# Chunk 0's statistics by quarters, two of its tiles staged by ScalarE, and transposes inside dense groups that read half of the chunk

## Chip, cores, metric

One core of one Trainium2 chip. The metric is the device time of one execution in microseconds; lower is better. Every timed comparison is of runs of two kernels on the same chip in the same rounds, with a 95% interval. Below, a "ratio" is the mean time of one kernel's runs over the mean of the other's runs of the same rounds; it is not quite the ratio of the medians that are quoted beside it. The record calls two kernels the same where they differ by less than 2%.

## The reference

Four residual layers over a sequence of 2048 tokens of width 1024, in bf16: a spectral layer (A) and a dense layer (B), twice.

```python
x = x + A(layernorm(x))      # rfft2 over (2048, 1024), times a complex filter, irfft2
x = x + B(layernorm(x))      # mish(x @ w1 + b1) @ w2, hidden width 3584
x = x + A(layernorm(x))
x = x + B(layernorm(x))
```

## The kernel before

Layer B works on four chunks of 512 tokens, each of four tiles of 128 tokens. What matters here is the passage from A to B, which occurs twice in an execution. In it, TensorE does the last stage of the inverse transform (`i4`, 128 small matmuls for tiles 0 to 3 and 128 for tiles 4 to 15), the results are added to the residual stream `XS` or staged in `YS`, VectorE takes the layer-norm statistics, scales a tile (`apply`), TensorE transposes it (`transposed`) and VectorE copies the transposed tile out of PSUM (the memory, in banks, into which TensorE writes) into `XT`, which the first product (`mm1`) then reads.

In these traces each engine keeps its program order: in the changed kernel below, the square root is ready to run at 620.08 us and starts at 620.51, behind ScalarE's own copies. The helper `op` makes an instruction wait for whatever wrote what it reads; `writes` also waits for earlier readers.

```python
def i4(self, lo, nb, u0, n, bank):          # n lanes of the inverse transform for nb tiles
    ...
    self.group(fns, reads=[... self.r_mt], writes=self.r_bank[bank:bank - (-n // k)])

def i4_out(self, lo, nb, u0, n, bank, staged=None):
    ...
    if staged is None:                      # VectorE adds PSUM to XS
        self.op(self.dve, ... tensor_tensor(xs, src, xs, ALU.add), reads=rb, parts=...)
    else:                                   # ScalarE copies PSUM to YS
        self.op(self.act, ... activation(dst, src, ACT.Copy), reads=rb, parts=[staged.res])

def transposed(c, t, xn, eng=None):
    bank = 6 + nt[0] % 2                    # banks 6 and 7 in turn
    ...                                     # 8 transposes of 128x128 into the bank
    self.op(eng or dve, fn, reads=[self.r_bank[bank]], parts=[XT[c % 2].res])

def mm1(c, fg, half=None):                  # 256 hidden columns; half: 256 of 512 tokens
    ...
    for fl in range(2):                     # banks 0 to 2 in turn
        ...
        self.group(fns, reads=[wb.res, x.res], writes=[self.r_bank[bank]])
        self.op(act, ... ACT.Mish ..., reads=[self.r_bank[bank], self.r_b1], writes=[ra])

# ---- the passage
for u in range(4):
    self.i4(0, 4, 32 * u, 32, 2 * u)
    self.i4_out(0, 4, 32 * u, 32, 2 * u)    # VectorE, four tiles at a time
rest(0)                                     # 15 lanes of tiles 4-15, banks 0-2, ScalarE stages
rest(3)                                     # the same in banks 3-5
self.stats_dve(0)
self.stats_dve(1)
for j in range(2):
    self.root(j, 1)                         # square root on ScalarE, reciprocal on VectorE
    xn[j] = self.apply(j)
rest(0)
late = rest(3, evac=False)
self.warm(ACT.Mish)                         # ScalarE's table load
for j in range(2):
    transposed(0, j, xn[j])
late()
...
for fg in range(4):
    mm1(0, fg, 0)
    rest(3)
for j in (2, 3):
    transposed(0, j, xn[j])
mm1(0, 0, 1)
rest(3)
...
mm1(0, 4)
for j in (4, 5):
    transposed(1, j - 4, xn[j])
...
for fg in range(2):
    mm1(1, fg, 0)
for j in (6, 7):
    transposed(1, j - 4, xn[j])
for fg in range(2):
    mm1(1, fg, 1)
# from here on full groups of mm1, then mm2; gapless
```

## Time and profile before

| | before |
|---|---|
| median of 3 runs, later of 4 | 1028.27 us, 1028.76 us |
| span of the profiled run | 1031.2 us |
| TensorE busy | 92% of the span |
| first passage: first `i4` matmul to first `mm2` matmul | 117.6 us |
| second passage | 120.3 us |

The passage is the measure I use throughout: the start of the first `mm2` matmul (L1024 before, L1046 in the changed kernel) less the start of the first `i4` matmul (L926 before, L939 after), read from TensorE's timeline. Before: 237.75 - 120.11 and 737.71 - 617.46. In a line of a timeline the first number is the start in us, the second the duration, then engine, line and operation, and in brackets the engine's idle time just before it and what ended it. The second passage's first group of `mm1`, 16 matmuls, in TensorE's timeline of the kernel before:

```profile
629.22 3.60 PE L1007 MATMUL PS<-ARENA 128*128 128x256 bf16 x16 [0.79 <-DVE ARENA L982]
```

The same group in the first passage (131.46 us) took 1.92 us: in the second the clock was at half. Where a text below says that the clock fell, the granted clock of short windows went from 1.00 to 0.50, for about 3.4 us ("one window") or about 6.8 us ("two windows", 627.3 to 634.1 us here). A waits line reads: who waited, for whom, us in total, times, longest.

### The profile page before, as it was taken

How to read it: one execution, taken by the hardware profiler on the slowest of the kernel's cores; microseconds unless marked ns; L12 is line 12 of the kernel's file. 1: busy time of each engine (PE TensorE's matmuls, PEld its weight loads, DVE VectorE, ACT ScalarE, POOL GpSimd, SP SyncE). 2: the span in 40 equal slices, each digit the busy share in tenths (PEclk: the TensorE clock that was granted, in tenths of full speed). 3: DMA queues.
4: the chain of work that ended last, by engine and by line, in shares of the span. 5: the costliest groups of instructions: out<-in, count | busy, mean ns of one | idle time of the engine just before them, and what ended most of it. 6: DMA issues, size and time to landing. Idle time of an engine off the chain costs nothing.

```text
span 1031.2 us, 13517 instructions
## 1 busy us (share of the span) xinstructions
PE 947.1 (92%) x5695; PEld 505.6 (49%) x5777; DVE 332.6 (32%) x682; ACT 348.5 (34%) x487; POOL 73.3 (7%) x114
## 2 busy tenths in 40 slices
PE   0799599999999999999979958999999999999998
PEld 0567475444444444444446747644444444444443
DVE  6897469002333100033346836840011100000111
ACT  6989384441000333300019846544200023330000
POOL 3342000000000000002511100000000000000000
PEclk9999799999999999999989988999999999999999
DMA  9879713653111220002932874155611122200000
GB/s 285 206 245 303 195 50 93 204 191 113 46 46 35 72 82 21 1 21 75 195 67 77 231 187 123 42 173 185 181 25 45 45 74 71 62 1 10 21 21 31
DMA packets 153052, 106.98 MB, mean 104 GB/s; under 512 B 74384, under 2 KB 132064, under 8 KB 152992
## 3 DMA queue, kind: packets, MB, share of 16 engines
q1 hardware_dynamic: 141472, 77.04, 26.4%
q0 software_dynamic: 9488, 27.68, 9.3%
q10 hardware_dynamic: 2032, 1.39, 0.5%
q8 instruction: 46, 0.75, 0.3%
q14 instruction: 14, 0.11, 0.0%
HBM read 80.85 MB, written 20.71 MB: 98 GB/s over the span
## 4 chain that ended last, share of the span: by engine, by line
PE 85%; DVE 7%; ACT 5%; DMA 2%; issue 1%; ACTq 0%; DVEq 0%
PE PS L1007 38%; PE PS L1024 37%; PE PS L676 2%; PE PS L750 2%; DVE BN L460 2%; PE PS L771 2%; ACT ARENA L601 2%; ACT ARENA L757 1%; ACT ARENA L728 1%; DVE XS L946 1%; PE PS L926 1%; DMA ARENA<-u_scratch 1%; DVE ARENA L982 1%; ACT ARENA L711 1%; PE PS L789 1%
## 5 line engine op out<-in xcount | busy, mean ns | idle before, releaser
L1007 PE MATMUL PS<-ARENA 128*128 128x512 bf16 (+1 forms) x1950 | 390.3, 359 | 9.0 <-DVE ARENA L982 7.2
L1024 PE MATMUL PS<-ARENA 128*128 128x512 bf16 x1756 | 385.5, 379 | 1.9
L1011 ACT ACTIVATE ARENA<-PS,B 128x512 bf16<-128x512 f32 (+1 forms) x248 | 159.3, 645 | 417.9 <-PE PS L1007 417.8
L1007 PEld LDWEIGHTS PS<-ARENA 128*128 128x128 bf16 x1984 | 193.9, 98 | 201.4 <-DVE ARENA L982 8.6
L1024 PEld LDWEIGHTS PS<-ARENA 128*128 128x128 bf16 x1792 | 175.4, 98 | 211.4
L1029 DVE TENSOR_TENSOR XS<-PS,XS 128x512 bf16<-128x512 f32 x64 | 44.3, 692 | 593.9 <-PE PS L1024 593.9
L460 DVE BATCH_NORM_STATS2 BN<-XS 128x6 f32<-128x512 bf16 x108 | 69.6, 674 | 7.5 <-DMA XS<-in_A_x_dram 6.4
L926 PE MATMUL PS<-MT,ARENA 128*128 128x32 bf16 (+1 forms) x512 | 22.2, 202 | 17.9 <-DMA ARENA<-u_scratch 15.6
L750 PE MATMUL PS<-ARENA 128*128 128x256 bf16 x256 | 32.3, 273 | 4.7 <-DVE ARENA L739 3.2
L676 PE MATMUL PS<-FD,ARENA 128*128 128x256 bf16 (+1 forms) x256 | 33.1, 278 | 3.8 <-DVE ARENA L603 1.5
L757 ACT ACTIVATE ARENA<-PS 128x1024 bf16<-128x1024 f32 x32 | 33.4, 1071 | 7.5 <-PE PS L750 7.5
L432 ACT ACTIVATE RS<-MV,EPS 128x1 f32<-128x1 f32 (+1 forms) x7 | 2.1, 295 | 100.0 <-DVE MV L463 96.4
L949 ACT ACTIVATE ARENA<-PS 128x1440 bf16<-128x1440 f32 (+2 forms) x20 | 25.0, 1274 | 28.1 <-PE PS L926 28.1
L728 ACT ACTIVATE ARENA<-PS 128x1024 bf16<-128x1024 f32 x32 | 33.0, 1061 | 4.0 <-PE PS L724 4.0
L249 POOL DMA_DIRECT2D xn_scratch<-ARENA x12 | 6.5, 541 | 378.5 <-DVE ARENA L499 378.5
L750 PEld LDWEIGHTS PS<-ARENA 128*128 128x128 bf16 x256 | 24.2, 98 | 12.6 <-DVE ARENA L739 4.6
L926 PEld LDWEIGHTS PS<-MT,ARENA 128*128 128x128 bf16 x512 | 20.3, 104 | 20.0 <-issue 15.9
L676 PEld LDWEIGHTS PS<-FD,ARENA 128*128 128x128 bf16 x256 | 25.1, 101 | 8.8 <-DVE ARENA L603 3.1
L771 PE MATMUL PS<-ARENA,BD 128*128 128x256 bf16 x192 | 27.1, 288 | 2.3 <-ACT ARENA L757 2.3
L732 DVE TENSOR_TENSOR ARENA<-ARENA 128x1024 bf16<-128x1024 bf16 x32 | 22.1, 689 | 20.8 <-ACT ARENA L728 20.8
L799 ACT ACTIVATE ARENA<-PS 128x1024 bf16<-128x1024 f32 x24 | 24.8, 1073 | 3.7 <-PE PS L771 3.7
L711 ACT ACTIVATE ARENA<-PS 128x1024 bf16<-128x1024 f32 x22 | 23.0, 1055 | 7.3 <-PE PS L676 7.3
(70 smaller groups left out, 499.2 us busy)
## 6 DMA issues: line engine op xcount, KB each, us to landing
ARENA<-in_B_w_dram SPq DMA_DIRECT2D x56, 512.0 KB, 4.0
ARENA<-in_B_w_dram SPq DMA_DIRECT2D x56, 256.0 KB, 4.4
u_scratch<-ARENA SPq DMA_DIRECT2D x14, 512.0 KB, 3.6
ARENA<-u_scratch SPq DMA_DIRECT2D x14, 512.0 KB, 5.7
XS<-in_A_x_dram SPq DMA_DIRECT2D x4, 1024.0 KB, 8.7
w_scratch<-ARENA POOLq DMA_DIRECT2D x8, 512.0 KB, 5.6
ARENA<-w_scratch POOLq DMA_DIRECT2D x8, 512.0 KB, 4.6
out_dram<-XS SPq DMA_DIRECT2D x16, 256.0 KB, 2.0
```

Source lines behind the costliest of these rows:

```text
L460: self.op(self.dve, lambda e: e.bn_stats(self.BN[:, j, 6 * h:6 * h + 6], self.XS[:, j, 512 * h:512 * h + 512]), reads=[self.r_xs[j]], part ...
L676: fns.append(lambda e: e.matmul(dst, at(r), FD[:, t:t + n], start=start, stop=stop))
L711: self.op(act, lambda e: e.activation(dst, src, ACT.Copy), reads=banks, parts=[za.res, zb.res])
L728: self.op(act, lambda e: e.activation(x.ap.rearrange("p a b -> p (a b)"), ps, ACT.Copy, scale=SIG), reads=banks, writes=[x.res])
L750: fns.append(lambda e, c=c, part=part: e.matmul(ps[:, c * 256:(c + 1) * 256], yk.ap[:, part, c * P:(c + 1) * P], t[:, (128, 0)[part]:(384, ...
L757: self.op(act, lambda e: e.activation(v.ap[:, :, i, :], src, ACT.Copy), reads=banks, parts=[v.res])
L771: fns.append(lambda e, dst=dst, part=part, c=c: e.matmul(dst, BD[:, c:c + P], mov(kd, part), start=(part == 0), stop=(part == 1)))
L926: fns.append(lambda e, l=l: e.matmul(self.PS[:, bank + l // k, l % k * w:(l % k + 1) * w], self.UT.ap[:, u0 + l, :], self.MT[:, 8 * lo:8 * ...
L1007: fns.append(lambda e, db=db, bank=bank, fl=fl: e.matmul(PS[:, bank, 0:w], wb.ap[:, db, fl * P:(fl + 1) * P], x.ap[:, db, tok], start=(db ...
L1011: self.op(act, lambda e, bank=bank, ft=ft: e.activation(at.ap[:, ft, tok], PS[:, bank, 0:w], ACT.Mish, bias=self.B1[:, ft:ft + 1]), reads= ...
L1024: fns.append(lambda e, i=i, ft=ft: e.matmul(PS[:, bank, :], at.ap[:, ft, t * P:(t + 1) * P], W2[ft].ap[:, h * 512:(h + 1) * 512], start=(i ...
L1029: self.op(dve, lambda e: e.tensor_tensor(xs, PS[:, bank, :], xs, ALU.add), reads=[self.r_bank[bank]], writes=[self.r_xs[j]])
```

## The change

The intent: have chunk 0's statistics ready sooner, by halving VectorE's adds (ScalarE stages tiles 2 and 3 in a new buffer `YC`) and taking statistics a quarter of the tile at a time between the adds; and let no copy of transposed tiles keep TensorE waiting, by putting the transposes into the middle of a group of matmuls that reads only the half of the chunk that is ready.

```diff
+    def stats_quarter(self, j, u):
+        ...
+        x = self.XS[:, j, :].rearrange("p (h l) -> p h l", l=P)[:, :, 32 * u:32 * u + 32]
+        self.op(self.dve, lambda e: e.bn_stats(bn[:, 6 * u:6 * u + 6], x), reads=[self.r_xs[j]], parts=[r])
+        if u == 3:
+            t = self.op(self.dve, lambda e: e.bn_aggr(self.MV[:, j, :], bn), reads=[r], writes=[r])
 ... (i4_out: tiles=, prog=; a staged copy now writes its banks' record)
-                self.op(self.act, lambda e, ...: e.activation(dst, src, ACT.Copy), reads=rb, parts=[staged.res])
+                self.copy(prog or self.act, at(staged.ap), src, [], rb, parts=[staged.res])
 ... (XT: one record for each half of the chunk)
-            self.op(eng or dve, fn, reads=[self.r_bank[bank]], parts=[XT[c % 2].res])
+            self.op(eng or dve, fn, reads=[self.r_bank[bank]], parts=[r_xt[c % 2][t // 2]])
-        def mm1(c, fg, half=None):
+        def mm1(c, fg, half=None, mid=()):
             for fl in range(2):
+                if fl:
+                    for f in mid:
+                        f()
-                self.group(fns, reads=[wb.res, x.res], ...)
+                self.group(fns, reads=[wb.res] + (r_xt[c % 2] if half is None else [r_xt[c % 2][half]]), ...)
 ... (the passage)
         for u in range(4):
             self.i4(0, 4, 32 * u, 32, 2 * u)
-            self.i4_out(0, 4, 32 * u, 32, 2 * u)
+            self.i4_out(0, 4, 32 * u, 32, 2 * u, tiles=(0, 2))
+            self.i4_out(0, 4, 32 * u, 32, 2 * u, staged=YC, tiles=(2, 2))
+            for j in range(2):
+                self.stats_quarter(j, u)
         rest(0)
+        self.root(0, 2)
         rest(3)
-        self.stats_dve(0)
-        self.stats_dve(1)
         for j in range(2):
-            self.root(j, 1)
             xn[j] = self.apply(j)
-        rest(0)
-        late = rest(3, evac=False)
-        self.warm(ACT.Mish)
         for j in range(2):
             transposed(0, j, xn[j])
-        late()
+        rest(3)
+        self.warm(ACT.Mish)
 ...
         for fg in range(4):
-            mm1(0, fg, 0)
+            mm1(0, fg, 0, mid=turns(0, 2, 3) if fg == 3 else ())
             rest(3)
-        for j in (2, 3):
-            transposed(0, j, xn[j])
+            if fg == 2:
+                rest(6, 10, dve)
         mm1(0, 0, 1)
-        rest(3)
+        rest(3, 13)
 ...
         mm1(0, 4)
         at_tiles(1)
-        for j in (4, 5):
-            transposed(1, j - 4, xn[j])
+        mm1(0, 5, mid=turns(1, 0, 1))
+        for ft in range(4):
+            load_w2(ft)
 ...
         for fg in range(2):
-            mm1(1, fg, 0)
-        for j in (6, 7):
-            transposed(1, j - 4, xn[j])
+            mm1(1, fg, 0, mid=turns(1, 2, 3) if fg else ())
         for fg in range(2):
             mm1(1, fg, 1)
 ... (mm1(1, 2) alone; loads of W2 and residual adds moved accordingly)
```

More of the change, by code (lines that the diff above doesn't have):

```diff
@@ L463, in stats_half @@
             self.op(self.dve, lambda e: e.bn_aggr(self.MV[:, j, :], self.BN[:, j, :]), reads=[r], writes=[r])
+    def stats_quarter(self, j, u):
+        r = self.r_mv[j]
+        if u == 0:
+            r.begin()
+        bn = self.BN[:, 2 * j:2 * j + 2, :].rearrange("p a b -> p (a b)")
+        x = self.XS[:, j, :].rearrange("p (h l) -> p h l", l=P)[:, :, 32 * u:32 * u + 32]
+        self.op(self.dve, lambda e: e.bn_stats(bn[:, 6 * u:6 * u + 6], x), reads=[self.r_xs[j]], parts=[r])
+        if u == 3:
+            t = self.op(self.dve, lambda e: e.bn_aggr(self.MV[:, j, :], bn), reads=[r], writes=[r])
+            for i in range(4):
+                self.r_mv[i].r(self.dve, t)
     def stats_dve(self, j):
@@ L533, in pair, with copy @@
         return self.PS[:, 2 * i:2 * i + 2, :].rearrange("p a b -> p (a b)"), [self.r_bank[2 * i], self.r_bank[2 * i + 1]], 2 * i
-    def copy(self, prog, dst, src, reads, writes, scale=None):
+    def copy(self, prog, dst, src, reads, writes, scale=None, parts=()):
         if prog is self.act:
@@ L541, in copy @@
             fn = lambda e: e.tensor_copy(dst, src)
-        return self.op(prog, fn, reads=reads, writes=writes)
+        return self.op(prog, fn, reads=reads, writes=writes, parts=parts)
     def first_scales(self):
@@ L928, in i4, with i4_out @@
         self.group(fns, reads=self.r_ut[u0 // 32:(u0 + n - 1) // 32 + 1] + [self.r_mt], writes=self.r_bank[bank:bank - (-n // k)])
-    def i4_out(self, lo, nb, u0, n, bank, staged=None):
+    def i4_out(self, lo, nb, u0, n, bank, staged=None, prog=None, tiles=None):
         w = 8 * nb
         k = 512 // w
+        t0, tn = tiles or (0, nb)
         for b0, m, i in ((0, n // k, k), (n // k, 1, n % k)):
@@ L937, in i4_out @@
                 continue
-            src = self.PS[:, bank + b0:bank + b0 + m, 0:i * w].rearrange("p b (i c) -> p c b i", c=w)
+            src = self.PS[:, bank + b0:bank + b0 + m, 0:i * w].rearrange("p b (i c) -> p c b i", c=w)[:, 8 * t0:8 * (t0 + tn)]
             l = slice(u0 + b0 * k, u0 + b0 * k + m * i)
@@ L944, in i4_out @@
             if staged is None:
-                xs = at(self.XS[:, lo:lo + nb, :])
-                self.op(self.dve, lambda e, src=src, xs=xs: e.tensor_tensor(xs, src, xs, ALU.add), reads=rb, parts=self.r_xs[lo:lo + nb])
-            else:
-                dst = at(staged.ap)
-                self.op(self.act, lambda e, src=src, dst=dst: e.activation(dst, src, ACT.Copy), reads=rb, parts=[staged.res])
+                j = slice(lo + t0, lo + t0 + tn)
+                xs = at(self.XS[:, j, :])
+                self.op(self.dve, lambda e, src=src, xs=xs: e.tensor_tensor(xs, src, xs, ALU.add), reads=rb, parts=self.r_xs[j])
+            else:
+                self.copy(prog or self.act, at(staged.ap), src, [], rb, parts=[staged.res])
     def load_w1(self, after=()):
@@ L963, in layer_B @@
         base = 28 * li
-        XT, AT, r_at = [None, None], [None, None], [None, None]
+        XT, AT, r_xt, r_at = [None, None], [None, None], [None, None], [None, None]
         nt, nh, no = [0], [0], [0]
@@ L972, in transposed @@
                 if XT[c % 2] is None:
-                    XT[c % 2] = self.alloc(f"XT{c % 2}", self.ob[f"XT{c % 2}"], [8, 512])
-                XT[c % 2].res.begin()
+                    off = self.ob[f"XT{c % 2}"]
+                    XT[c % 2] = self.alloc(f"XT{c % 2}", off, [8, 512])
+                    r_xt[c % 2] = self.sub_res(XT[c % 2], f"xt{c % 2}h", 2, off, 8192)
+                for r in r_xt[c % 2]:
+                    r.begin()
             fns = []
@@ L989, in turned @@
             if t == 0:
-                x.res.begin()
+                for r in r_xt[c % 2]:
+                    r.begin()
             for db in range(8):
                 self.dma(sp, x.ap[:, db, t * P:(t + 1) * P], xn.ap[:, db * P:(db + 1) * P], f"xt{c % 2}_{t}", reads=[xn.res],
-                         parts=[x.res], transpose=True)
-        def mm1(c, fg, half=None):
+                         parts=[r_xt[c % 2][t // 2]], transpose=True)
+        def mm1(c, fg, half=None, mid=()):
             n = base + 14 * (c // 2) + fg
@@ L1008, in mm1 @@
                         PS[:, bank, 0:w], wb.ap[:, db, fl * P:(fl + 1) * P], x.ap[:, db, tok], start=(db == 0), stop=(db == 7)))
-                self.group(fns, reads=[wb.res, x.res], writes=[self.r_bank[bank]])
+                self.group(fns, reads=[wb.res] + (r_xt[c % 2] if half is None else [r_xt[c % 2][half]]), writes=[self.r_bank[bank]])
                 at, ra = AT[c % 2], r_at[c % 2][ft]
@@ L1059, in layer_B @@
         YS.res.begin()
+        YC = self.alloc("YC", self.ob["XT1"], [2, self.D])
+        YC.res.begin()
         xn = {}
-        for j in range(4):
+        for j in range(2):
             self.r_xs[j].begin()
@@ L1070, in at_tiles, with rest, turns @@
                 self.live.append((off + ft * 1024, off + ft * 1024 + 1024, r))
-        def rest(bank, evac=True):
-            u0, n = self.u0, min(15, P - self.u0)
+        def rest(bank, n=15, prog=act):
+            u0 = self.u0
             self.u0 += n
             self.i4(4, 12, u0, n, bank)
-            out = lambda: self.i4_out(4, 12, u0, n, bank, staged=YS)
-            if not evac:
-                return out
-            out()
+            self.i4_out(4, 12, u0, n, bank, staged=YS, prog=prog)
         def residual(j):
-            self.op(dve, lambda e: e.tensor_tensor(self.XS[:, j, :], self.XS[:, j, :], YS.ap[:, j - 4, :], ALU.add),
-                    reads=[YS.res], writes=[self.r_xs[j]])
+            y, i = (YS, j - 4) if j > 3 else (YC, j - 2)
+            self.op(dve, lambda e: e.tensor_tensor(self.XS[:, j, :], self.XS[:, j, :], y.ap[:, i, :], ALU.add),
+                    reads=[y.res], writes=[self.r_xs[j]])
+        def turns(c, *ts):
+            return [lambda t=t: transposed(c, t, xn[4 * c + t]) for t in ts]
         self.u0 = 0
@@ L1090, in layer_B @@
             self.i4(0, 4, 32 * u, 32, 2 * u)
-            self.i4_out(0, 4, 32 * u, 32, 2 * u)
+            self.i4_out(0, 4, 32 * u, 32, 2 * u, tiles=(0, 2))
+            self.i4_out(0, 4, 32 * u, 32, 2 * u, staged=YC, tiles=(2, 2))
+            for j in range(2):
+                self.stats_quarter(j, u)
         rest(0)
+        self.root(0, 2)
         rest(3)
-        self.stats_dve(0)
-        self.stats_dve(1)
         for j in range(2):
-            self.root(j, 1)
             xn[j] = self.apply(j)
-        rest(0)
-        late = rest(3, evac=False)
-        self.warm(ACT.Mish)
         for j in range(2):
             transposed(0, j, xn[j])
-        late()
+        rest(3)
+        self.warm(ACT.Mish)
         at_tiles(0)
-        self.stats_dve(2)
-        self.stats_dve(3)
+        for j in (2, 3):
+            residual(j)
+            self.stats_dve(j)
         self.scales(2, 2)
@@ L1138, in layer_B @@
         for fg in range(2):
-            mm1(1, fg, 0)
-        for j in (6, 7):
-            transposed(1, j - 4, xn[j])
+            mm1(1, fg, 0, mid=turns(1, 2, 3) if fg else ())
         for fg in range(2):
             mm1(1, fg, 1)
-        w2_order = list(range(16)) + list(range(16, 28))
-        for fg in range(5, 14 + 3):
+        mm1(1, 2)
+        w2_order = list(range(4, 28))
+        for fg in range(6, 14 + 3):
             if fg < 14:
@@ L1149, in layer_B @@
             mm1(1, fg - 3)
-            if fg < 9:
-                for j in (2 * fg - 2, 2 * fg - 1):
+            if fg < 10:
+                for j in (2 * fg - 4, 2 * fg - 3):
                     residual(j)
```

## The prediction

> **What bounds the kernel now.** I read the page first (shares of busy time, then the chain), then the chain in order of time to find the stretches in which TensorE does not set the end, then the timelines of TensorE, VectorE and ScalarE there, then the granted clock in short windows.
>
> The page: TensorE (PE) is busy for most of the span, and the two lines of the dense layer hold three quarters of the chain.
>
> ```profile
> PE 947.1 (92%) x5695; PEld 505.6 (49%) x5777; DVE 332.6 (32%) x682; ACT 348.5 (34%) x487; POOL 73.3 (7%) x114
> PE PS L1007 38%; PE PS L1024 37%; PE PS L676 2%; PE PS L750 2%; DVE BN L460 2%; PE PS L771 2%; ACT ARENA L601 2%; ACT ARENA L757 1%; ACT ARENA L728 1%; DVE XS L946 1%; PE PS L926 1%; DMA ARENA<-u_scratch 1%; DVE ARENA L982 1%; ACT ARENA L711 1%; PE PS L789 1%
> ```
>
> The change touches only the passage from the spectral layer to the dense layer, twice per execution (from 120 us and from 617 us). The chain through the first passage (start, length, what):
>
> ```profile
> 120.11 1.03 PE PS L926 x32
> 121.16 4.63 DVE XS L946 x4
> 125.82 1.30 DVE BN L460 x2
> 127.35 1.16 DVE BN L460 x2
> 128.97 1.64 ACT ARENA L949
> 130.63 1.28 ACT L425
> 132.13 1.27 ACT ARENA L949
> ...
> 141.90 1.30 DVE ARENA L982 x2
> ...
> 154.88 1.30 DVE ARENA L982 x2
> 156.23 3.67 PE PS L1007 x32
> 160.38 1.30 DVE ARENA L982 x2
> ```
>
> The reader sees four adds (L946), the statistics of tiles 0 and 1 (L460), ScalarE's evacuations and its table load, and then three times 1.30 us in which VectorE copies two transposed tiles (L982) while TensorE has nothing to do. TensorE's waits from 113 to 240 us confirm the last point:
>
> ```profile
> PE PS L1007 <- DVE ARENA L982: 3.6, 4, 0.9
> ```
>
> TensorE's own timeline gives the durations I use below:
>
> ```profile
> 133.45 0.81 PE L926 MATMUL PS<-MT,ARENA 128*128 128x96 bf16 x15
> 134.09 1.91 PE L1007 MATMUL PS<-ARENA 128*128 128x256 bf16 x16
> 154.22 1.08 PE L977 MATMUL PS<-IDENT,ARENA 128*128 128x128 bf16 x16
> ```
>
> Start to start, 15 lanes of the remaining inverse transform ("a rest", L926) take 0.64 us (43 ns a lane), a half group of 16 matmuls of 256 columns takes 1.75 us, a full one 3.46 us (16 of 216 ns: 49 take 10.74 us less the drain), and two tiles of transposes 0.92 us. From about 165 us on TensorE is gapless (72.6 of 73 us), so only these passages can give. All useful TensorE work between 120.1 and 165.2 us is about 38 us, so even a perfect passage would save some 7 us, 14 us in both: under 1.5%.
>
> The second passage repeats the first but is 2.6 us longer by the time chunk 0's second half starts (643.22 - 617.46 against 143.24 - 120.11). The reason is the clock:
>
> ```profile
> 625.00:627.00 2.00, 0.67 (x15) 0.53 (x13) 1.89 (x7) 0.90 (x3) 0.00 (x0) 1.00 1.16 311
> 627.00:629.00 2.00, 1.41 (x15) 0.96 (x12) 1.56 (x3) 1.98 (x2) 0.00 (x0) 0.58 1.18 299
> 629.00:631.00 2.00, 1.78 (x9) 1.28 (x10) 1.97 (x5) 1.73 (x3) 0.00 (x0) 0.50 0.93 236
> 631.00:633.00 2.00, 2.00 (x14) 1.50 (x13) 1.78 (x8) 0.62 (x2) 0.00 (x0) 0.50 0.06 17
> ```
>
> After a thin stretch (0.67 us of TensorE in two) the clock (column before the DMA share) falls to 0.50 and the first matmul groups run at half speed.
>
> **What the Trainium skill says.** (1) "TensorE: Matmul & The Clock Gate", Part 1: full clock after a busy window of about 3.4 us, half clock after an idle one, in windows that run freely. The trace agrees on both passages (0.50 at the first matmuls, the fall at 627.3, the rise near 634.1, two windows apart), except that here a window need not be idle to cost the clock: I count about 1.3 us of work in the one before 627.3. (2) "VectorE: DVE Perf Modes", section on the errata: an fp32 tensor_tensor takes (N+151)/0.96 ns. The trace: 1216 ns for N = 1024, 692 for 512, so halving the add halves little less than its time. (3) "ScalarE: Activation LUTs", What ACT_TABLE_LOAD costs: 186 + 0.833 N ns with overlap of about 93; the trace has 1408 ns for 1440 elements and 592 for 480, so about 0.62 us for 512. (4) "PSUM — Partial Sum Buffer", Terms: two engines on one bank at once collide. No run here shows it, but the diff obeys it: an evacuation now writes its bank's record, so ScalarE's copy of tiles 2 and 3 waits until VectorE's add of tiles 0 and 1 has left the same banks.
>
> **Part 1: statistics by quarters.** Removed from VectorE: two of the four tiles in each of four adds (1.16 us each start to start), and the statistics after them (4 of 0.65 us and two aggregations). Added: four adds of 512 elements, 0.69 us + 0.03 to the dependent instruction; eight statistics of 256 elements, about 0.41 us each by itself (674 ns less 256/0.96) and 0.35 start to start. A quarter cycles in 0.72 + 2 x 0.35 = 1.42 us. Add number 3 starts at 121.16 + 3 x 1.42 = 125.44 and ends at 126.13; the last aggregation ends near 127.4, against 128.74: 1.35 us earlier. But ScalarE is a strict queue: its fourth staged copy can start only at 126.17, then comes the rest's evacuation (about 1.25 start to start) and only then the square root: 126.17 + 0.54 + 1.25 = 127.96, not 127.4. Reciprocal, scaling: first transpose at 129.05 against 129.40, second tile's copy ends at about 131.05, first matmul group at 131.10 against 131.46. Of 1.35 us some 0.36 remain.
>
> **Part 2: one rest goes behind the transposes and before the table load.** Its evacuation can start at 130.75 and ends at 132.2; table load and warm-up end at 133.65; Mish 0 ends at 134.1, Mish 1 at 134.5, and the next evacuation at 135.9. TensorE, through with groups 0 and 1 at 135.25, waits for that bank set until 135.95 (0.7 us lost). The kernel before is at the same place at 135.84, with one rest more behind it in fact, though the new one gives ten lanes to VectorE later. The 0.36 us are gone.
>
> **Part 3: chunk 0's tiles 2 and 3 inside group 3.** The wait of 0.94 us at 143.24 goes: the last rest (0.64) and half a group lie over the copies. But the ten lanes for VectorE use banks 6 and 7, which the transposes need next. From 139.43: copy of 960 elements about 1.16 us, from 139.6 to 140.77, while TensorE has only 0.87 us of work to 140.3: it waits 0.5. Then 0.92 + 0.87 + 0.64 us: chunk 0's second half starts at 143.24, as before. The last rest has 13 lanes instead of 8: +0.21, so 145.55 against 145.34.
>
> **Part 4: chunk 1's transposes inside groups.** Before: the two waits for VectorE's copy after 154.22 and 159.73 cost 1.09 and 1.11 us, and the transposes themselves wait 0.16 us. After: from 145.55, three half groups 5.24, full groups 4 and 5 6.92, two tiles 0.92, two half groups 3.50, two tiles 0.92: 163.05; the last copy is done about 0.2 us later: 163.25. Before, this point is 161.72 with full group 5 (3.46) still to do: 165.18. Saved 1.93 us in each passage. The tiles are ready in time: 4 and 5 at 154.2 for 156.0, 6 and 7 at about 160.9 for 161.2. The first W1 reload is issued at 165.0, takes about 4.0 us (median landing) and is needed at 170.2: hidden. The early W2 loads and the moved residual adds lie beside dense matmuls.
>
> **Clock.** The new order leaves TensorE idle from about 126.1 to 129.05. Any window over that is thin, so I expect a fall to half clock in both passages, where before it fell in one of the two. Following one such fall through parts 2 and 3: if it comes before the transposes, the serial ScalarE part starts about 1.4 us later; if it comes after them, group 0 loses 1.7 us and 0.7 of it replaces the wait of part 2. So about 1.3 us a passage, 2.6 for both, against 2.6 before: no net change.
>
> **Sum.** 1028.27 - 2 x 1.93 = 1024.4 us.
>
> **The rivals.** First: the gain stays in the opening as well (ScalarE's queue is not in the way). For it: the statistics do end 1.35 us earlier. Against: the evacuation precedes the root in program order. It would make 2 x (1.93 + about 1.0): 1022.4. Second: the clock decides. For it: an idle stretch of 3 us; the trace has a fall after a thinner gap. Against: a second cold window only helps ScalarE catch up. If each passage lost 2.6: 1027. Third: the W1 reload arrives late because the slack before it shrinks from 8.6 to 5.2 us, with 4.0 to land; a late one would add up to 1 us a passage: 1026. Fourth: the transpose copies were hidden behind something else; but the chain itself runs through all three, so I give it little.
>
> **Range and chances.** My terms for ScalarE's order and for the bank 6 and 7 wait may each be off by 0.5 us a passage, and the clock by 1 us: 1021.5 to 1027.6. More than 2% (20 us) exceeds all idle time of both passages, so faster gets 1%; slower by 20 us would need a stall that nothing here shows, 0.5%.
>
> **What would show it.** Right: no wait of L1007 for the copies of L982 after the first of each passage; the root's start set by ScalarE's own queue after the evacuation; a wait of about 0.7 us of a rest for ScalarE before group 2; transposes of tiles 2 and 3 waiting about 0.5 us for VectorE; PEclk of 0.5 near 129 and its like in the second passage. Wrong: transposes inside the groups waiting for the scaling; a matmul waiting for in_B_w; the dense part starting later than 165 us.

## The result and the profile after

| | before | after |
|---|---|---|
| median (range) | 1028.76 us (1027.05 to 1030.16, 4 runs) | 1025.24 us (1024.37 to 1026.31, 4 runs) |
| ratio | | 0.9967, 95% interval 0.9948 to 0.9986 |
| span of the profiled run | 1031.2 us | 1022.6 us |
| first passage | 117.64 us | 116.11 us |
| second passage | 120.25 us | 116.25 us |

A gain of about 3.4 us by the ratio (0.0033 x 1028.8). The two profiled spans differ by more, 8.6 us. Of that, 2.7 us lie before the first passage (it starts at 117.39 us instead of 120.11), where nothing was changed; a second trace of the kernel before, told below, starts it at 117.50 us, so this was the one run. The passages hold 1.5 and 4.0 us, the large one against a passage of before that had lost its clock for long.

The page of the changed kernel, its line of engines and its chain by lines: the dense lines (now L1046 and L1029) have the same shares.

```profile
PE 948.8 (93%) x5777; PEld 504.5 (49%) x5777; DVE 334.4 (33%) x694; ACT 350.2 (34%) x491; POOL 72.3 (7%) x114
...
PE PS L1046 38%; PE PS L1029 37%; PE PS L689 2%; PE PS L763 2%; ACT ARENA L614 2%; PE PS L784 2%; DVE BN L460 1%; PE PS L939 1%; ACT ARENA L770 1%; ACT ARENA L741 1%; ACT ARENA L724 1%; PE PS L995 1%; DMA ARENA<-u_scratch 1%; ACT ARENA L550 1%; PE PS L802 1%; DMA XS<-in_A_x_dram 1%
```

The chain of the changed kernel through its second passage (start, length, what; L961 is VectorE's add, L472 its statistics by quarters, L550 ScalarE's plain copies, L432 the root, L995 the transposes, L425 the table load, L554 VectorE's copy of ten lanes, L1000 the copies of transposed tiles):

```profile
614.63 0.75 DVE BN L472 x2
...
618.14 0.60 DVE XS L961
...
618.76 1.86 ACT ARENA L550 x2
620.62 0.19 ACT RS L432
...
621.65 1.20 PE PS L995 x16
...
624.08 1.66 ACT ARENA L550
...
625.76 1.28 ACT L425
...
632.96 1.17 DVE ARENA L554
...
634.18 1.07 PE PS L995 x16
...
655.20 1.30 DVE ARENA L1000 x2
...
656.54 7.55 PE PS L1029 x50
```

The reader is to see, against the chain of before, that the statistics after the fourth add have left it: it goes straight to two ScalarE copies and the root. The statistics between the adds are in it, three times 0.75 us of L472 (the first is shown). Statistics end at 620.08, the root starts at 620.51, behind ScalarE's own queue. Then come the third rest's evacuation and the table load, also ScalarE's. Of the copies of transposed tiles that stood in the chain of before (three in its first passage, four in this one) only the last is left, and it ends about 0.2 us after TensorE's work.

TensorE's waits from 600 to 740 us of the changed kernel:

```profile
PE PS L995 <- DVE ARENA L512: 2.8, 1, 2.8
...
PE PS L939 <- ACT ARENA L550: 1.0, 3, 0.6
PE PS L995 <- DVE ARENA L554: 0.4, 1, 0.4
```

The 3.6 us for the copies are gone. The longest wait inside the passage is now that of the first transposes for the scaled tiles (L512), 2.8 us, and after it the clock falls. Short windows of the changed kernel (window, its length, busy us of TensorE, its weight loads, VectorE, ScalarE and GpSimd, then the granted clock, DMA share, GB/s):

```profile
620.00:622.00 2.00, 0.35 (x7) 0.36 (x8) 1.20 (x4) 2.00 (x3) 0.00 (x0) 1.00 1.18 314
622.00:624.00 2.00, 2.00 (x29) 1.99 (x27) 1.74 (x4) 0.15 (x1) 0.00 (x0) 0.61 1.18 294
624.00:626.00 2.00, 2.00 (x12) 1.44 (x10) 1.93 (x5) 1.90 (x2) 0.00 (x0) 0.53 1.16 280
```

### The profile page after: what moved, and what is told of

It reads as the page before. It is cut to its first block, busy times and chain, and to the rows that moved or that the text cites. A ratio compares the mean times of both kernels' runs of the same rounds, so it can differ in the third digit from the quotient of the medians.

```text
span 1022.6 us, 13611 instructions
## 1 busy us (share of the span) xinstructions
PE 948.8 (93%) x5777; PEld 504.5 (49%) x5777; DVE 334.4 (33%) x694; ACT 350.2 (34%) x491; POOL 72.3 (7%) x114
## 4 chain that ended last, share of the span: by engine, by line
PE 85%; ACT 6%; DVE 6%; DMA 2%; issue 0%; ACTq 0%; DVEq 0%
PE PS L1046 38%; PE PS L1029 37%; PE PS L689 2%; PE PS L763 2%; ACT ARENA L614 2%; PE PS L784 2%; DVE BN L460 1%; PE PS L939 1%; ACT ARENA L770 1%; ACT ARENA L741 1%; ACT ARENA L724 1%; PE PS L995 1%; DMA ARENA<-u_scratch 1%; ACT ARENA L550 1%; PE PS L802 1%; DMA XS<-in_A_x_dram 1%
## 5 line engine op out<-in xcount | busy, mean ns | idle before, releaser
L1029 PE MATMUL PS<-ARENA 128*128 128x512 bf16 (+1 forms) x1984 | 393.1, 360 | 0.1
L1046 PE MATMUL PS<-ARENA 128*128 128x512 bf16 x1792 | 387.4, 379 | 0.0
L1029 PEld LDWEIGHTS PS<-ARENA 128*128 128x128 bf16 x1984 | 194.2, 98 | 193.8 <-DVE ARENA L1000 0.9
L1046 PEld LDWEIGHTS PS<-ARENA 128*128 128x128 bf16 x1792 | 175.3, 98 | 211.4
L460 DVE BATCH_NORM_STATS2 BN<-XS 128x6 f32<-128x512 bf16 x100 | 64.7, 676 | 7.5 <-DMA XS<-in_A_x_dram 6.3
L550 ACT ACTIVATE ARENA<-PS 128x1440 bf16<-128x1440 f32 (+3 forms) x26 | 28.0, 1095 | 27.9 <-DVE XS L961 23.3
L432 ACT ACTIVATE RS<-MV,EPS 128x2 f32<-128x2 f32 (+2 forms) x5 | 1.5, 298 | 97.5 <-DVE MV L463 96.2
```

The lines of the kernel that those rows point to most:

```text
L460: self.op(self.dve, lambda e: e.bn_stats(self.BN[:, j, 6 * h:6 * h + 6], self.XS[:, j, 512 * h:512 * h + 512]), reads=[self.r_xs[j]], part ...
L550: fn = (lambda e: e.activation(dst, src, ACT.Copy)) if scale is None else \
L1029: fns.append(lambda e, db=db, bank=bank, fl=fl: e.matmul(PS[:, bank, 0:w], wb.ap[:, db, fl * P:(fl + 1) * P], x.ap[:, db, tok], start=(db ...
L1046: fns.append(lambda e, i=i, ft=ft: e.matmul(PS[:, bank, :], at.ap[:, ft, t * P:(t + 1) * P], W2[ft].ap[:, h * 512:(h + 1) * 512], start=(i ...
```

## The experiments

Twelve runs were made, all with correct results: eleven variants and the kernel before once more. Each was to isolate a term of the prediction's sum. All timed runs are in the fast state; the kernel before once more is a single run, whose state is unknown, and only its trace is used. The ratio is always to the kernel before; the changed kernel's own is 0.9967. The variants ran on three chips, so two of them are compared only through these ratios.

| run | median us | ratio (95% interval) | passages us |
|---|---|---|---|
| changed kernel | 1025.24 | 0.9967 (0.9948 to 0.9986) | 116.11, 116.25 |
| only the last part | 1026.10 | 0.9965 (0.9950 to 0.9980) | 116.88, 117.99 |
| only the opening | 1029.86 | 1.0008 (0.9995 to 1.0020) | 118.71, 119.63 |
| chunk 0 transposed after the group | 1026.58 | 0.9976 (0.9960 to 0.9991) | 117.47, 117.03 |
| statistics by halves | 1025.42 | 0.9961 (0.9948 to 0.9974) | 117.72, 115.66 |
| root first | 1025.53 | 0.9967 (0.9955 to 0.9980) | 117.08, 116.65 |
| ten lanes early | 1023.00 | 0.9947 (0.9934 to 0.9960) | 115.93, 115.62 |
| dummies in the gap | 1023.27 | 0.9943 (0.9929 to 0.9957) | 116.31, 115.57 |
| table load early | 1024.97 | 0.9954 (0.9942 to 0.9967) | 114.90, 117.08 |
| ten lanes and table early | 1023.95 | 0.9941 (0.9922 to 0.9960) | 115.23, 116.54 |
| all three | 1020.47 | 0.9914 (0.9900 to 0.9927) | 114.47, 114.18 |
| all three, more dummies | 1021.80 | 0.9931 (0.9911 to 0.9951) | 114.18, 114.18 |
| before again | 1029.87 (1 run) | | 118.10, 119.19 |

The passages of one trace carry two accidents: whether the clock fell and for how long, and, in most first passages, a wait of up to 1.1 us of the second quarter for data from memory. The wait occurs in the second trace of the kernel before as well, so it is not the change's. Where a passage decides something below, I say which and compare like with like.

### Only the last part

```diff
 # changed kernel, with the opening of the kernel before put back:
-            self.i4_out(..., tiles=(0, 2)); self.i4_out(..., staged=YC, tiles=(2, 2)); stats_quarter ...
+            self.i4_out(0, 4, 32 * u, 32, 2 * u)
 ...
-            mm1(0, fg, 0, mid=turns(0, 2, 3) if fg == 3 else ())
+            mm1(0, fg, 0)
 ... (transposes of tiles 2 and 3 after group 3, table load and rests as before)
 # kept: mm1(0, 5, mid=turns(1, 0, 1)), mm1(1, 1, 0, mid=turns(1, 2, 3)), half records of XT
```

> The kernel before with only the last part of the change: chunk 1's transposes inside full group 5 and inside half group 1, its matmuls reading their half of the chunk; the opening (statistics by halves, four tiles added by VectorE, chunk 0's transposes after group 3) is as before. Theory A (the prediction): the gain is the two waits of about 1.1 us in each passage, so this has all of it: ratio to before 0.9963, about 1025, no wait for the transposes' copies after the third one. Theory B (the opening, with its statistics 1.35 us earlier, gives half of it): ratio 0.998, about 1026.9. A passage, from its first inverse-transform matmul to the first matmul of the second product, is 117.6 us before where the clock holds and 120.3 where it falls: A expects 115.7 and 118.3, B 116.7 and 119.3.

It gave 1026.1 us, ratio 0.9965. Theory A's 0.9963 is well inside the interval and theory B's 0.998 at its edge, so the trace decides. Its second passage lost the clock for two windows, as that of the kernel before did, so the two compare directly: 117.99 against 120.25, a gain of 2.26 us, where theory A had 118.3 and theory B 119.3. TensorE's waits from 605 to 740 us in this kernel:

```profile
PE PS L1029 <- DVE ARENA L1000: 1.7, 2, 0.9
```

Two waits for copies of transposed tiles are left, both in the old opening; the two of chunk 1 are gone.

### Only the opening

```diff
         at_tiles(1)
-        mm1(0, 5, mid=turns(1, 0, 1))
-        for ft in range(4):
-            load_w2(ft)
+        for f in turns(1, 0, 1):
+            f()
 ...
-            mm1(1, fg, 0, mid=turns(1, 2, 3) if fg else ())
+            mm1(1, fg, 0)
+        for f in turns(1, 2, 3):
+            f()
 ... (mm1(0, 5) and the four loads behind mm1(1, 1, 1))
```

> The changed kernel with chunk 1's transposes put back between the groups and full group 5 put back behind them; the opening stays new. Theory A: the two waits of about 1.1 us come back in each passage, nothing else does, ratio to before 1.000 (about 1028.8), passages 1.9 us longer than in the changed kernel (118.0 and 118.2). Theory B: ratio 0.998, about 1026.9. Together with the run of the other part, the two should add up to the whole change (0.9967) if the parts do not interact.

It gave 1029.86 us, ratio 1.0008: theory A again, theory B outside the interval. The two parts add up to 0.9973, and the whole is 0.9967: within the intervals they add. TensorE's waits from 113 to 240 us in this kernel:

```profile
PE PS L1029 <- DVE ARENA L1000: 2.2, 3, 0.9
```

So the new opening as a whole is worth nothing that the time shows: by the interval it lies between 0.5 us gained and 2.1 us lost. The next runs ask why, since its statistics did become quicker.

### Chunk 0's transposes after the group

```diff
-            mm1(0, fg, 0, mid=turns(0, 2, 3) if fg == 3 else ())
+            mm1(0, fg, 0)
             rest(3)
             if fg == 2:
                 rest(6, 10, dve)
+        for f in turns(0, 2, 3):
+            f()
```

> The changed kernel with chunk 0's tiles 2 and 3 transposed after the fourth group and its rest, as before. Theory A: the wait for the copies of the transposed tiles comes back (0.94 us) and the wait of the transposes for the ten lanes goes (0.38 us), so each passage is 0.56 us longer (116.7 to 116.8 where the clock fell as in the changed kernel), total 1026.3. Rival (the wait of the transposes inside the group is worth as much as the one it replaced): no difference, 1025.2.

1026.58 us against 1025.24, near the 1026.3 expected; the intervals of the two ratios overlap, so the verdict rests on the waits (second passage, 605 to 740 us), where the old wait is back and that for the ten lanes is gone from the list:

```profile
PE PS L1029 <- DVE ARENA L1000: 0.9, 1, 0.9
```

This part of the opening thus gains about half a microsecond a passage. The second passage is 0.78 us longer than the changed kernel's; the other 0.2 us is a wait for W1 from memory. Since the opening as a whole gains nothing, something else in it seems to give this back; that is within the noise of its time.

### Statistics by halves

```diff
             self.i4_out(0, 4, 32 * u, 32, 2 * u, staged=YC, tiles=(2, 2))
-            for j in range(2):
-                self.stats_quarter(j, u)
+        for j in range(2):
+            self.stats_dve(j)
         rest(0)
```

> The changed kernel with the statistics of tiles 0 and 1 taken as before, by halves of a tile after the fourth add (each add still two tiles, the other two staged by ScalarE). Theory A (the strict queue on ScalarE already sets the root's start, so quarters as such buy little): the last aggregation ends about 0.6 us later, the first transposes only 0.1 to 0.3 us later (about 9.0 us after the first inverse-transform matmul instead of 8.8), total 1025.2 to 1025.8, not to be told from the changed kernel. Rival (the quarters are what makes the opening quicker): transposes 0.6 us or more later and total 1026.5.

Theory A has the time, which is that of the changed kernel (0.9961), but neither has the second passage, which had no wait for memory in either kernel. The first transposes did not come later there: they came 8.38 us after the first `i4` matmul (623.04 - 614.66), in the changed kernel 8.79 (621.65 - 612.86). Two lines of ScalarE's timeline in this run, and one of TensorE's:

```profile
618.95 1.86 ACT L550 ACTIVATE ARENA<-PS 128x512 bf16<-128x512 f32 x2 [0.21 <-DVE XS L961]
621.91 0.29 ACT L432 ACTIVATE RS<-MV,EPS 128x2 f32<-128x2 f32 x1 [1.10 <-DVE MV L463]
```

```profile
623.04 1.08 PE L995 MATMUL PS<-IDENT,ARENA 128*128 128x128 bf16 x16 [3.44 <-DVE ARENA L512]
```

The last aggregation of the statistics (VectorE's timeline), first in this run and then in the changed kernel:

```profile
621.66 0.21 DVE L463 BATCH_NORM_AGGREGATE MV<-BN 128x2 f32<-128x12 f32 x1
```

```profile
619.81 0.27 DVE L474 BATCH_NORM_AGGREGATE MV<-BN 128x2 f32<-128x24 f32 x1
```

Without statistics between them the four adds end sooner, ScalarE's fourth staged copy starts 4.29 us after the first `i4` matmul instead of 5.90 (618.76 - 612.86), the evacuation behind it is out of the way, and the root waits for the statistics. In this passage the quarters do not end the statistics any sooner: the end is 7.21 us after the first `i4` matmul with halves and 7.22 with quarters. They only stretch the adds, and so hold up ScalarE's copies, which the root stands behind. Each order is bound by the other engine.

The first passages say something else. They wait for memory before the second add, and where that wait is the same, 1.08 us, the transposes come 9.69 us after the first `i4` matmul with halves and 9.53 with quarters (the run with dummies below). So in a first passage the quarters gain 0.16 us, in a second one they lose 0.41, and the time shows neither.

### Root first

```diff
-        rest(0)
         self.root(0, 2)
+        rest(0)
         rest(3)
```

> The changed kernel with the square root queued on ScalarE ahead of the first remaining evacuation. Theory A (ScalarE's strict queue swallowed most of the earlier statistics): the root starts when the last aggregation ends, 0.4 us sooner, the first transposes 0.4 us sooner after the first inverse-transform matmul (8.5 us instead of 8.9), and the passage is up to 0.4 us shorter, 1024.5 in all. Rival: the half clock that follows the idle stretch decides, and what comes 0.4 us sooner is lost again before group 2: passages as in the changed kernel, 1025.2.

In the second passage the transposes did start 0.4 us sooner (8.39 us, 622.26 - 613.87, the same as with halves), as theory A has it, but the passage was not shorter (116.65) and the ratio is the changed kernel's, 0.9967. The rival has the time right. The evacuations behind the root came later for it (the second one 8.7 us after the first `i4` matmul, in the changed kernel 7.8), and TensorE waited 0.5 us for one before group 2.

### Ten lanes early

```diff
-            if fg == 2:
+            if fg == 1:
                 rest(6, 10, dve)
```

> The changed kernel with the ten lanes that VectorE evacuates from banks 6 and 7 moved from behind group 2 to behind group 1. Theory A (the transposes of tiles 2 and 3 wait 0.38 us for that evacuation to free their banks): the wait goes, each passage is 0.38 us shorter, 1024.5 in all. Rival: the evacuation, now ahead of the last rests, makes TensorE wait elsewhere (VectorE still busy with the scaling of tiles 2 and 3, or ScalarE behind by a group), and the passages stay at 116.1 and 116.2.

The wait went, as two lines of TensorE's timeline show (no bracket at the transposes, where the changed kernel had 0.38 us):

```profile
631.81 1.04 PE L1029 MATMUL PS<-ARENA 128*128 128x256 bf16 x8
632.68 1.06 PE L995 MATMUL PS<-IDENT,ARENA 128*128 128x128 bf16 x16
```

The second passage took 115.62 us instead of 116.25, and the time was 1023.0 us (0.9947). The wait that went accounts for 0.8 us in both passages; the measured 2 us against the changed kernel are more, but the intervals overlap (0.9934 to 0.9960 and 0.9948 to 0.9986), and I leave the rest open.

### Dummies in the gap

```diff
+        self.group([lambda e: e.matmul(self.PS[:, 7, :], self.IDENT[:], self.FD[:, 0:512], start=True, stop=True)] * 9,
+                   reads=[self.r_ident, self.r_fd], writes=[self.r_bank[7]])
         for j in range(2):
             transposed(0, j, xn[j])
```

> The changed kernel with nine dummy matmuls of 512 columns on bank 7 in the 2.8 us in which TensorE waits for tiles 0 and 1 (constants as operands, result never read). Theory A (the idle stretch costs the clock in each passage, some 0.6 to 1.3 us net): no short window of either passage below full clock between the dummies and the dense part, group 0 as 16 matmuls in about 1.92 us instead of 2.9 to 3.2, then a wait of about 0.7 us for ScalarE before group 2 appears; passages about 0.6 us shorter, total 1024.0. Rival (clock loss is hidden by ScalarE's serial table load and evacuations, so it costs nothing): passages at 116.1 and 116.2, total 1025.2.

The clock held in both passages once it had risen, the first group took 1.92 us, and the wait for ScalarE came out from behind it, as predicted (TensorE's timeline, second passage):

```profile
623.22 1.92 PE L1029 MATMUL PS<-ARENA 128*128 128x256 bf16 x16 [0.29 <-DVE ARENA L1000]
...
628.19 0.81 PE L939 MATMUL PS<-MT,ARENA 128*128 128x96 bf16 x15 [0.50 <-ACT ARENA L550]
```

The passage was 0.7 us shorter than the changed kernel's second (115.57), the time 1023.27 us (0.9943). The intervals of the two ratios overlap, but the record lists the mean granted clock of every run, traced or not: 0.987 in all five with the dummies, 0.982 or 0.983 in the four of the changed kernel, and from 0.982 to 0.987 in those of the kernel before. By this measure the dummies held the clock in every run. A fall thus costs something even here, though a wait for ScalarE's queue took the place of a part of it.

### Table load early

```diff
-        rest(3)
         self.warm(ACT.Mish)
+        rest(3)
```

> The changed kernel with ScalarE's table load queued ahead of the third remaining evacuation, into 1.5 us in which ScalarE waits for TensorE. Theory A: ScalarE is then ready 1.4 us sooner for the first activations, but TensorE at half clock is the slower of the two there, so alone it saves only the 0.2 us wait for ScalarE in the second passage: total 1025.0. Rival (ScalarE's queue is what sets the start of group 2 in both passages): 1 us a passage, total 1023.2.

1024.97 us, as expected. Its trace has both cases side by side: the first passage kept its clock by the luck of the windows and took 114.9 us, the second fell for two windows and took 117.08: about 2.2 us for this longer fall.

### All three, and all three without the dummies

The ten lanes behind group 1, the table load ahead of the third rest, and the dummies in the gap, in one kernel; then the same without the dummies.

> The changed kernel with the ten lanes moved behind group 1, the dummies in the gap and the table load ahead. Theory A (the opening is bound by clock and ScalarE's queue together; removing both makes TensorE dense from the first group on): group 1 starts 13.1 us after the first inverse-transform matmul instead of 14.4, no waits of TensorE after the first group, passages about 114.5, total about 1021.7. If the clock costs nothing, it stays at 1023.0, where the ten lanes alone were.

> The ten lanes behind group 1 and the table load ahead, but no dummy matmuls, so that the difference to the kernel with all three (1020.5) is the clock alone. Theory: where a passage keeps its clock it takes 114.5 us as with dummies; where it falls, ScalarE no longer hides it and it takes 116.5 to 117; total 1022.5 to 1023. Rival (clock loss hidden anyway): 1020.5.

All three together gave 1020.47 us (1019.58 to 1021.40), ratio 0.9914 (0.9900 to 0.9927): faster than the changed kernel, whose interval it does not touch, and than the kernel before. The passages are 114.47 and 114.18 us, and TensorE waits for nothing between the first group and the dense part. Two pieces of its chain in the second passage, the last copies of transposed tiles there and the group behind them:

```profile
619.88 1.30 DVE ARENA L1000 x2
...
621.22 1.92 PE PS L1029 x16
```

Without the dummies it is 1023.95 us, 0.9941: by the ratios the clock alone is 2.8 us of time ((0.9941 - 0.9914) x 1029). Their intervals just overlap (0.9922 to 0.9960 is the second), so the passages are the better measure: none of these three waited for memory, and against 114.18 us a fall for one window cost 1.05 us (115.23, first passage) and one for two windows 2.36 us (116.54, second). In the second the same group took 3.40 us (TensorE's timeline):

```profile
624.68 3.40 PE L1029 MATMUL PS<-ARENA 128*128 128x256 bf16 x16
```

No run put the dummies into the kernel before, or into the one with only the last part. How much of the 1020.47 us needs the new opening, and how much the dummies would give without it, is not shown.

### More dummies, before the passage

Twelve more dummy matmuls at the start of layer B, while TensorE waits for memory.

> All three fixes, and in addition twelve dummy matmuls ahead of each passage, while TensorE waits for the transposed data from memory, so that the passage starts at full clock. Theory: 128 matmuls of 32 columns take about 3.5 instead of 4.1 us, but VectorE's quarters of 1.4 us set the pace there, so only the first add comes some 0.15 us sooner: passages 114.0 to 114.2 and total 1020.2, not to be told from 1020.5. Rival (cold start is on the path): 113.5 and 1019.2.

A miss in its premise, the start at full clock. They ran at full clock right behind the spectral layer's last matmuls (12 in 2.76 us), left TensorE idle for 4.8 and 5.9 us, and the passage began at half clock as ever. Passages are the same (114.18 both), the time 1021.8 us (0.9931), with one run of 1025.8; the intervals of the two overlap. Whether a longer row of dummies that reaches up to the data would help was not tried.

### The kernel before, once more

> The kernel before once more, unchanged, for a second trace: its passages should be about 117.6 us where the clock stays up and 120.3 us where it falls for two windows, with something between for one; the waits for the copies of transposed tiles (3 of 0.9 us on TensorE in the later part) should be the same to 0.1 us.

The first passage kept its clock and took 118.10 us, of which 0.58 us was the wait for memory: 117.5 without it, as expected. The second fell for one window (119.19). The waits for the copies were 3.6 us, 4 times, in both. So of four traced passages of the kernel before two lost the clock, of the changed kernel's two both did.

## Why the prediction was right, point by point

The time predicted was 1024.4 us, measured 1025.24; the predicted saving of 3.9 us was measured as 3.4.

- **Part 4, the transposes of chunk 1, holds the whole gain.** Right. It was put at 1.93 us a passage. Alone it gave 2.26 us in the comparable passage (without the longer last rest, 0.21 us, that the whole change adds) and 3.6 us in the time. The 0.2 us wait of the last copy is in the chain of the changed kernel. The time of the whole change fixes its gain only to about 2 us either way (0.9948 to 0.9986).
- **Part 1, the quarters.** The opening step was right for the reason given: the root stands behind ScalarE's queue. The statistics end 7.22 us after the first `i4` matmul, 1.4 us sooner than before (626.09 - 617.46 = 8.63), as predicted. The transposes were predicted 8.94 us after the first `i4` matmul, measured 8.79; the kernel before has 9.29 in the second passage. The quarter's cycle was put at 1.42 us and is 1.38. But the prediction credited the quarters with the sooner statistics and transposes. The halves show otherwise: with the two tiles staged by ScalarE, plain halves end the statistics as soon (7.21), and the transposes come sooner still in a second passage (8.38), 0.16 us later in a first one that waits for memory. The staging helps; the quarters as such are not shown to. Two small slips of the working changed nothing: 121.16 + 3 x 1.42 is 125.42, and 1408 ns is a median over copies of three sizes, while a copy of 1440 elements takes 1444 ns in the mean.
- **Part 2, the wait for ScalarE before group 2.** Put at 0.7 us. It is 0.50 and 0.58 us where the clock holds (the dummies' run) and 0 to 0.17 us in the changed kernel, where it falls once the transposes have begun, since a slow first group covers the wait. Where it fell before the transposes and had risen by the first group (first passage of the run with chunk 0's transposes after the group), the wait was there, 0.58 us: the two cases that the prediction set apart.
- **Part 3, the ten lanes' banks.** Put at 0.5 us, measured 0.38, and it goes when the ten lanes move up. That the opening nets to zero agrees with its run (1.0008, 0.9995 to 1.0020).
- **The clock.** That it would fall in both passages was right in the trace. That it makes no net change is consistent with the total, whose interval is too wide to test it; the sizes were off. The estimate was 1.3 us a fall; 0.7 us is what the traced second passage gained from the dummies, and with the ten lanes and the table load moved a fall cost 1.05 us for one window and 2.36 for two. How many windows a fall lasts differs from run to run. In so far as these sizes cancelled, the nearness of 1024.4 to 1025.24 is luck.
- **The rivals.** The first (the opening gains as well) fell with the run of the opening alone. The second (the clock decides) is true only of the improved kernels. The third (the W1 reload comes late) did not happen in the changed kernel; it shows once, as 0.2 us, in the second passage of the run with chunk 0's transposes after the group.

## What to carry to other kernels

Putting a transpose into the middle of a group of matmuls that does not need it hides the copy behind it for the price of a second record for half a tile; here it was worth all of the change that the times show. Before making one engine's result ready sooner, look at the queue of the engine that uses it next, and at whether the interleaving delays something that stands ahead in that queue. And when one wait is removed, look at what stood behind it: the dummies that hold the clock brought a wait of 0.5 us for ScalarE to light, and with the early table load and the ten lanes moved as well TensorE kept its clock and waited for nothing from the first group on, 5.5 us faster than the changed kernel by the ratios (0.9967 - 0.9914). The times do not show that the three need each other: alone they gave 2.5, 1.3 and 2.1 us by the ratios (0.9943, 0.9954 and 0.9947 against 0.9967), 5.9 together.

## What the Trainium skill lacked or had wrong

- "TensorE: Matmul & The Clock Gate", Part 1: the clock is said to fall after an idle window. In the kernel before it fell at about 627.3 us although TensorE was busy for 1.5 us of the 3.4 us before (the prediction counted 1.3); in the changed kernel 0.8 us of work in the 3.4 us before 622.5 us went ahead of a fall. How thin a window has to be is not on the page, which also tells of falls from frequent short idle times but gives no measure, and these runs do not settle it.
- The same page, Part 4: PE-mode transposes are said not to engage the full clock. Here 16 transposes of 128 x 128 take 1.06 to 1.08 us at full clock and 1.89 us at half (second passage of the run with the table load early), so they run at whichever clock is granted (whether they count as work that raises the clock, as the page doubts, was not tested); start to start in a dense stretch they take 0.89 us, 56 ns each.
- "VectorE: DVE Perf Modes" has no row for the batch-norm statistics. Measured: 674 ns for 512 elements, 0.37 to 0.43 us for 256, and for the aggregation 0.21 us of two groups and 0.26 us of four.
